# Cross attention and a PReLU layer on one core: small matmul bursts moved to the bank changes, ScalarE's long passes two units apart, batch 1's chain begun in unit 1

## The chip, the cores and the metric

The kernel runs on one core of one Trainium2 chip. The metric is the device time of one execution in microseconds (us), as the median of several runs. All times below are us, unless they are marked ns.

A core has five engines that run side by side and wait for one another by semaphores: TensorE (matmuls, shown as PE, its weight loads as PEld), VectorE (DVE), ScalarE (ACT), GpSimd (POOL) and SyncE (SP, which here only issues DMAs). Each engine works through its own list in order.

## What is computed

Eight batches of cross attention between 512 tokens `x` and 32 states, eight heads of 64, in both directions, and then one layer with a parametric ReLU over all rows:

```python
scores = scale * x @ state.T            # per batch and head: 512 x 32
xread  = softmax(scores) @ state        # the tokens read the states
sread  = softmax(scale * state @ x.T) @ x   # the states read the tokens
rows   = concatenate([xread, sread], axis=2)   # 544 rows of 512 per batch
h      = rows @ w_in                    # d_ff = 2048
g      = maximum(h, 0) + alpha * minimum(h, 0)
out    = g @ w_out
```

Inputs and outputs are float32; the kernel's matmuls take float16.

## The kernel before, in words

**Units.** The main loop (line 546) runs over 128 units, u = 16·b + jc: batch b of 8, block jc of 16 blocks of 128 columns of d_ff. "Relative unit" n of batch b below means u = 16·(b − 1) + n, as in the diff, where the chain of batch b is spread over the units of the batch before. In a unit three things are put into the engines' lists, in this order:

1. `first(b, jc)` (line 363): the first product for the 512 tokens of the batch, two matmuls of 512 columns (L369). `w_in` isn't applied to the token rows: for each batch the product of the states and `w_in`, called m, is made ahead (`state_w_in`, `m_matmuls`, L337, copied by ScalarE, L351), and the softmax weights aT multiply m. Then ScalarE makes `neg`, a relu of −h (L386), and VectorE adds `(1 − alpha)·neg` to h (L391). Its result is gt, the input of the second product. h lies in one of three PSUM buffers (`ps_h`), so a first product waits until the gt of three units before has been made.
2. Some steps of `second` (line 397), the product with `w_out` (L401). Each of a batch's four blocks of 128 tokens, q = 0 to 3, is summed over all 16 jc in a PSUM bank of its own. There are two such banks (`ps_o`), so q = 0 and 1 run together, then 2 and 3. A bank is reused when ScalarE has copied it out (L412, osb); SyncE sends osb to memory. From unit 18 on, a unit holds four matmuls of it, and a pair of banks is finished every eight units, at u = 18, 26, 34 and so on.
3. The side work that `at(u, ...)` has put there (lines 451 to 508): the order is written out by hand.

**The side work of a batch.** `load_x` (GpSimd's DMA, L76); the transpose of x, for batches 0 and 1 by TensorE (`x_transposed_pe`, four transposes and a copy, L167, L170), later by a DMA on SyncE's queue (L158); `scores` (16 small matmuls, L179); for the tokens' softmax `score_blocks` (VectorE transpose, L209), `state_max` (L217), `state_shift` (GpSimd, L223), `state_exp` (ScalarE, L229), `state_sum` (L234, L235), `state_norm` (GpSimd, L238) and `weights_back` (VectorE transpose, L246); for the states' softmax `token_max` (L258, L261), two `token_exp` (ScalarE, L269) and a DMA transpose (L279), `state_reads` (32 small matmuls, L291, and two VectorE operations), `state_reads_transposed` (two transposes, L313, and four VectorE copies into XS, L320); and four `state_w_in`, f = 0 to 3, eight matmuls of 64 rows by 32 columns of weights each. The small matmuls of one such step are called a burst.

**PSUM.** Eight banks: three for h, two for the second product, two as one buffer (`ps_two`) which `scores` and `state_w_in` share, and one (`ps_misc`) for the transposes and state reads. So a `state_w_in` that follows scores waits until both `token_exp` have read them.

**Batch 8.** The states' rows of all batches are the last first product, `first(B, jc)` (L378), four matmuls of 256 columns on XS. In the kernel before, it is done in units 112 to 127, one jc each; after the loop the rest of `second` and `second_reads` (L423) follow.

**Before the loop** (lines 510 to 545) batch 0's chain is done, and GpSimd issues the loads of `w_in` (four parts), `w_out` (four parts) and x(1), x(2) on one queue.

Of the kernel before, what the change touches and what calls it, by code (L numbers as in the profile page):

```python
# [8 lines left out]
F32 = mybir.dt.float32  # L9
# [8 lines left out]
def kernel(  # L18
# [33 lines left out]
    moe = ctx.enter_context(tc.tile_pool(name="moe", bufs=2))  # L52
# [63 lines left out]
    def st_head(b, h):  # L116
        return stT[:, N * (H * b + h) : N * (H * b + h + 1)]
# [72 lines left out]
    def blocks(t):  # L190
        return t.rearrange("p (a n) -> p a n", n=N)

    def over_blocks(t):
        return t.unsqueeze(2).to_broadcast([128, t.shape[1], N])


    def cols(t, j, n):
        return t if j is None else t[:, n * j : n * (j + 1)]
# [22 lines left out]
    def state_shift(b, engine, j=None):  # L221
        ts = blocks(cols(live["ts", b], j, S))
        engine.tensor_tensor(  # L223
            ts, ts, over_blocks(cols(live["mx", b], j, S // N)), ALU.subtract
        )
# [102 lines left out]
    def m_tile(b):  # L328
        if b not in ms:
            ms[b] = moe.tile([128, n_f, 2, 512], F16, name=f"m_{b}", tag="m", bufs=B - 1)  # L330
        return ms[b]

    def m_matmuls(t, b, f, g):
        for k in range(4):
            h = 4 * g + (k ^ g)
            c, r = divmod(h, 2)
            nc.tensor.matmul(  # L337
                t[N * k : N * (k + 1), :],
                st_head(b, h)[64 * r : 64 * r + 64, :],
                w_in_sb[64 * r : 64 * r + 64, c, 512 * f : 512 * (f + 1)],  # L340
                start=True,
                stop=True,
                tile_position=(64 * r, N * k),
                skip_group_check=True,
            )

    def state_w_in(b, f):
# [2 lines left out]
            m_matmuls(t[:, g, :], b, f, g)  # L350
        nc.scalar.copy(m_tile(b)[:, f, :, :], t)  # L351

    def state_w_in_early(b, f):
        ts = [ps_h(f"m_ps{b}_{f}_{g}", [128, 512], F32) for g in range(2)]
        for g in range(2):
            m_matmuls(ts[g], b, f, g)
        for g in range(2):
            nc.scalar.copy(m_tile(b)[:, f, g, :], ts[g])


    gts = {}
# [32 lines left out]

    outs = {}

    def second(b, half, jc):
        for q in (2 * half, 2 * half + 1):
            if jc == 0:
                outs[b, q] = ps_o(f"o_{b}_{q}", [128, d_model], F32)  # L400
            nc.tensor.matmul(  # L401
                outs[b, q],
                gts[b, jc][:, 128 * q : 128 * (q + 1)],
                w_out_sb[:, jc, :],
                start=(jc == 0),
                stop=(jc == n_jc - 1),
            )
        if jc < n_jc - 1:
            return
        for q in (2 * half, 2 * half + 1):  # L410
            osb = moe.tile([128, d_model], F32, name=f"osb_{b}_{q}", tag="osb", bufs=3)
            nc.scalar.copy(osb, outs.pop((b, q)))  # L412
            r, j = divmod(q, 2)
            rows = out[b * S2 : b * S2 + S, :].rearrange("(j p r) d -> r j p d", j=2, r=2)
            nc.sync.dma_start(rows[r, j], osb)


    def second_reads(q):
# [15 lines left out]
            (nc.scalar if i == 0 else nc.sync).dma_start(rows[:, :, w * i : w * (i + 1)], osb)  # L434


    seconds = [(b, half, jc) for b in range(B) for half in range(2) for jc in range(n_jc)]


    def seconds_before(u):  # L440
        if u >= 18:
            return 2 * (u - 10)
        return max(0, u - 3) + (1 if u >= 16 else 0)

    side = {}

    def at(u, fn, *a):
        side.setdefault(u, []).append((fn, a))

    vcopy, acopy = nc.vector.tensor_copy, nc.scalar.copy  # L450
    at(0, states_rest_out, 1)
    at(1, token_exp, 0, 0)
    at(2, token_exp, 0, 1)
    at(3, state_w_in, 0, 2)
    at(5, state_w_in, 1, 0)
    at(4, x_transposed_pe, 1, 0, 0, ps_misc, vcopy)
    at(5, x_transposed_pe, 1, 0, 1, ps_misc, acopy)
    at(6, x_transposed_pe, 1, 1, 0, ps_misc, vcopy)
    at(6, x_transposed_pe, 1, 1, 1, ps_h, acopy)
    at(7, scores, 1)  # L460
    at(8, score_blocks, 1)
    at(9, state_max, 1)
    at(9, state_shift, 1, nc.gpsimd)
    at(9, state_w_in_early, 0, 3)
    at(10, token_max, 1)
    at(11, token_exp, 1, 0)
    at(11, state_exp, 1)
    at(12, token_exp, 1, 1)
    at(12, state_sum, 1)
    at(12, state_norm, 1, nc.gpsimd)  # L470
    at(13, state_w_in, 1, 1)
    at(14, weights_back, 1)
    at(14, token_exp_transposed, 0)
    at(14, x_transposed, 2)
    at(15, state_w_in, 1, 2)
    at(17, token_exp_transposed, 1)
    at(19, state_reads, 0)
    at(21, state_reads_transposed, 0)
    at(22, load_x, 3)
    at(23, state_w_in, 1, 3)  # L480
    for b in range(2, B):
        u = n_jc * (b - 1)
        at(u, scores, b)
        at(u + 1, score_blocks, b)
        at(u + 2, state_max, b)
        at(u + 2, state_shift, b, nc.gpsimd)
        at(u + 3, token_max, b)
        at(u + 4, token_exp, b, 0)
        at(u + 5, state_exp, b)
        at(u + 6, token_exp, b, 1)  # L490
        at(u + 6, state_sum, b)
        at(u + 6, state_norm, b, nc.gpsimd)
        at(u + 7, token_exp_transposed, b)
        if b + 1 < B:
            at(u + 7, x_transposed, b + 1)
        at(u + 9, weights_back, b)
        for f in range(n_f):
            at(u + (9 if b == 2 else 8) + 2 * f, state_w_in, b, f)
        if b == 2:
            at(u + 8, state_reads, 1)  # L500
            at(u + 9, state_reads_transposed, 1)
            at(u + 10, load_x, 4)
        at(u + 11, state_reads, b)
        at(u + 14, state_reads_transposed, b)
        if b + 3 < B:
            at(u + 15, load_x, b + 3)
    for jc in range(n_jc):
        at(n_jc * (B - 1) + jc, first, B, jc)

    states_transposed_first()  # L510
    x_transposed_pe(0, 0, 0, ps_h, vcopy)
# [8 lines left out]
    state_max(0, 1)  # L520
    for f in range(2):
        load_w_in(f)
    load_w_out(0)
    load_w_in(2)
    load_x(1)
    load_w_out(1)
    state_shift(0, nc.gpsimd, 0)
    load_w_in(3)
    load_w_out(2)
    state_shift(0, nc.vector, 1)  # L530
    states_transposed_rest()
    state_exp(0, 0)
    state_exp(0, 1)
    state_w_in_early(0, 0)
    states_rest_out(0)
    state_sum(0, 0)
# [3 lines left out]
    state_sum(0, 1)  # L540
    state_norm(0, nc.vector, 1)
    state_w_in_early(0, 1)
    weights_back(0, 0)
    weights_back(0, 1)
    token_max(0)
    for u in range(n_jc * B):
        first(*divmod(u, n_jc))
        for sec in seconds[seconds_before(u) : seconds_before(u + 1)]:
            second(*sec)
        for fn, args in side.get(u, ()):  # L550
            fn(*args)
    for sec in seconds[seconds_before(n_jc * B) :]:
        second(*sec)
# [32 lines left out]
```

## Time and profile before

| | us |
|---|---|
| median of 3 runs | 245.57 (245.49 to 247.1) |
| the profiled execution | 245.95 |
| its span, first to last instruction | 244.1 |
| TensorE busy | 217.4 (89%) |
| VectorE busy | 170.8 (70%) |
| ScalarE busy | 149.8 (61%) |
| GpSimd busy | 46.1 (19%) |
| second product, L401 | 134.1 in 512 matmuls |
| first product, L369 | 78.6 in 256 matmuls |

A row of a timeline gives start, length, engine, line, operation, result and operands, the shape, and how many instructions are merged in it; in brackets stands how long the engine had been idle and what released it. Matmuls are pipelined: a row's length is longer than the distance from one start to the next, so the distances of starts are what counts. "Clock" is the share of TensorE's full clock that was granted. A table by stage gives, for each stretch of time, the busy time of each engine with the count of its instructions.

### The profile page before, as it was taken

Reading aid. Unit: us, or ns where it says so; the run is one execution under the profiler, and the core shown is the slowest. Engines: PE = TensorE matmul, PEld = TensorE weight load, DVE = VectorE, ACT = ScalarE, POOL = GpSimd, SP = SyncE. Lnnn points to the kernel's source line nnn. Section 1 sums busy time; section 2 is a strip of 40 time slices with the busy share of each in tenths; the row PEclk is TensorE's granted clock in tenths of the full one; section 3 lists DMA queues with packets and bytes.
Section 4 is the critical chain, followed back from the end, with each engine's and each line's share of the span. In section 5 each row is a group of like instructions: output and inputs, shape, how many; then the busy total and the mean of one; then the engine's idle time right before and its main releaser. Section 6 shows DMA issues by size and latency. Waiting matters only on the chain.

```text
span 244.1 us, 4170 instructions
## 1 busy us (share of the span) xinstructions
PE 217.4 (89%) x1632; PEld 97.7 (40%) x1632; DVE 170.8 (70%) x264; ACT 149.8 (61%) x261; POOL 46.1 (19%) x40
## 2 busy tenths in 40 slices
PE   0848867988999999999999999999999999999891
PEld 0513322333344334433444344434443455554381
DVE  0796687779969767977797778787878777673000
ACT  2378766658575965596559665966586675753100
POOL 8850033054203220313031102120212000000000
PEclk9999997999999999999999999999999999999998
DMA  9999997268992358238822602260212020202031
GB/s 79 192 203 195 196 175 89 87 86 119 199 118 86 70 155 78 86 31 192 85 86 45 173 1 86 38 180 0 90 30 99 3 87 0 86 3 83 3 124 51
DMA packets 49363, 23.12 MB, mean 95 GB/s; under 512 B 40512, under 2 KB 45248, under 8 KB 49344
## 3 DMA queue, kind: packets, MB, share of 16 engines
q0 software_dynamic: 20896, 8.62, 28.5%
q1 hardware_dynamic: 26096, 13.96, 21.8%
q10 hardware_dynamic: 2352, 0.27, 0.9%
q8 instruction: 13, 0.21, 0.4%
q14 instruction: 6, 0.05, 0.1%
HBM read 17.31 MB, written 8.91 MB: 107 GB/s over the span
## 4 chain that ended last, share of the span: by engine, by line
PE 65%; DVE 10%; ACT 8%; DMA 6%; issue 5%; POOL 3%; ACTq 0%; DVEq 0%; POOLq 0%
PE o L401 36%; PE h L369 17%; DMA xg<-in_x_dram 6%; ACT osb L412 4%; DVE gt L391 4%; PE m_ps L337 4%; PE o L423 3%; PE h L378 3%; ACT neg L386 2%; PE sc L179 1%; DVE ts L209 1%; DVE nb L258 1%; DVE r L234 1%; DVE mx L217 1%; POOL w_in_sb L98 1%
## 5 line engine op out<-in xcount | busy, mean ns | idle before, releaser
L401 PE MATMUL o<-w_out_sb,gt 128*128 128x512 f16 x512 | 134.1, 381 | 3.5 <-ACT osb L412 2.0
L391 DVE SCALAR_TENSOR_TENSOR gt<-neg,oma_sb,h 128x512 f16<-128x512 f32 x128 | 92.6, 735 | 35.8 <-ACT neg L386 34.8
L386 ACT ACTIVATE neg<-h 128x512 f32<-128x512 f32 (+1 forms) x144 | 82.4, 579 | 40.1 <-PE h L369 29.9
L369 PE MATMUL h<-aT,m 128*128 128x512 f16 x256 | 78.6, 392 | 2.2 <-DVE aT L246 1.7
L401 PEld LDWEIGHTS <-gt 128*128 128x128 f16 x512 | 50.3, 98 | 68.7 <-issue 11.9
L351 ACT CAST m<-m_ps 128x1024 f16<-128x1024 f32 x29 | 29.4, 1013 | 13.8 <-PE m_ps L337 13.3
L369 PEld LDWEIGHTS <-m 128*128 128x128 f16 x256 | 22.0, 99 | 26.7 <-issue 10.1
L223 POOL TENSOR_TENSOR ts<-ts,mx 128x1024 f32<-128x1024 f32 (+1 forms) x8 | 14.4, 1799 | 90.3 <-DVE mx L217 90.3
L412 ACT COPY osb<-o 128x512 f32<-128x512 f32 x32 | 17.2, 595 | 8.3 <-PE o L401 7.8
L238 POOL TENSOR_TENSOR an<-ts,r 128x1024 f16<-128x1024 f32 (+1 forms) x8 | 14.4, 1803 | 37.6 <-DVE r L235 32.9
L337 PE MATMUL m_ps<-w_in_sb,stT 64*32 64x512 f16 x256 | 14.0, 406 | 7.2 <-ACT e L269 5.2
L269 ACT ACTIVATE e<-sc,nb 128x512 f16<-128x512 f32 x16 | 11.1, 692 | 11.2 <-DVE nb L261 11.2
L320 DVE COPY XS<-srT_ps 64x64 f16<-64x64 f16 x32 | 14.1, 439 | 0.6
L337 PEld LDWEIGHTS <-stT 64*32 64x32 f16 x256 | 4.0, 89 | 21.1 <-issue 19.4
L76 POOL DMA_DIRECT2D xg<-in_x_dram x9 | 10.3, 1142 | 10.4 <-PE sr_ps L291 6.3
L433 DVE COPY osr<-o 128x256 f32<-128x256 f32 x2 | 0.8, 424 | 16.2 <-PE o L423 16.2
L391 DVE SCALAR_TENSOR_TENSOR gs<-neg,oma_sb,h 128x256 f16<-128x256 f32 x16 | 7.7, 480 | 5.6 <-ACT neg L386 5.6
L246 DVE STREAM_TRANSPOSE aT<-an 128x1024 f16<-128x1024 f16 (+1 forms) x9 | 10.0, 1119 | 1.7 <-POOL an L238 1.7
L217 DVE TENSOR_REDUCE mx<-ts 128x32 f32<-128x1024 f32 (+1 forms) x9 | 9.8, 1091 | 0.1
L229 ACT ACTIVATE ts<-ts 128x1024 f32<-128x1024 f32 (+1 forms) x9 | 8.6, 959 | 2.0 <-POOL ts L223 1.5
L234 DVE TENSOR_REDUCE r<-ts 128x32 f32<-128x1024 f32 (+1 forms) x9 | 9.8, 1088 | 0.0
L258 DVE TENSOR_REDUCE nb<-sc 128x2 f32<-128x1024 f32 x8 | 9.7, 1210 | 0.0
(41 smaller groups left out, 98.4 us busy)
## 6 DMA issues: line engine op xcount, KB each, us to landing
out_dram<-osb SPq DMA_DIRECT2D x32, 256.0 KB, 2.2
xg<-in_x_dram POOLq DMA_DIRECT2D x7, 512.0 KB, 7.6
w_in_sb<-in_moe_w_in_dram POOLq DMA_DIRECT2D x4, 512.0 KB, 11.1
w_out_sb<-in_moe_w_out_dram POOLq DMA_DIRECT2D x4, 512.0 KB, 18.4
xg<-in_x_dram POOLq DMA_DIRECT2D x2, 256.0 KB, 4.9
out_dram<-osr ACTq DMA_DIRECT2D x2, 128.0 KB, 2.8
out_dram<-osr SPq DMA_DIRECT2D x2, 128.0 KB, 2.8
st<-in_state_dram POOLq DMA_DIRECT2D x1, 224.0 KB, 5.3
```

The lines of the kernel that those rows point to most:

```text
L217: nc.vector.tensor_reduce(cols(live["mx", b], j, S // N), blocks(cols(live["ts", b], j, S)), AX.X, ALU.max)
L223: engine.tensor_tensor(ts, ts, over_blocks(cols(live["mx", b], j, S // N)), ALU.subtract)
L234: nc.vector.tensor_reduce(r1, blocks(cols(live["ts", b], j, S)), AX.X, ALU.add)
L238: engine.tensor_tensor(blocks(cols(live["an", b], j, S)), blocks(cols(live["ts", b], j, S)), over_blocks(cols(live["r1", b], j, S // N)), ...
L320: nc.vector.tensor_copy(XS[64 * r : 64 * r + 64, 2 * g : 2 * g + 2, :, b], t[64 * r : 64 * r + 64, 4 * g + (r ^ g) : 4 * g + 4 : 2, :],)
L337: nc.tensor.matmul(t[N * k : N * (k + 1), :], st_head(b, h)[64 * r : 64 * r + 64, :], w_in_sb[64 * r : 64 * r + 64, c, 512 * f : 512 * (f ...
L351: nc.scalar.copy(m_tile(b)[:, f, :, :], t)
L369: nc.tensor.matmul(h.rearrange("p (r j s) -> p r j s", r=2, j=2), ms[b][:, f, g, 128 * j : 128 * (j + 1)], weights(b, g), start=(g == 0), ...
L386: nc.scalar.activation(neg, h, RELU, bias=0.0, scale=-1.0)
L391: nc.vector.scalar_tensor_tensor(gt, neg, oma_sb[:, jc : jc + 1], h, ALU.mult, ALU.add)
L401: nc.tensor.matmul(outs[b, q], gts[b, jc][:, 128 * q : 128 * (q + 1)], w_out_sb[:, jc, :], start=(jc == 0), stop=(jc == n_jc - 1),)
L412: nc.scalar.copy(osb, outs.pop((b, q)))
```

## The change

- The order of `second`. Before, the two banks of a half took turns by jc. Now `second` does one q and one jc, in the same turns, but for the first and last two jc of a half: there both jc of one q come first, then both of the other. Each q is copied out right after its own last matmul. In the early units the second product starts at unit 7 in place of 3, with two or four matmuls per unit, and has done the same 32 by unit 18.
- The side work of batches 2 to 7 moves within the 16 units: `scores` from relative unit 0 to 1, with `state_reads_transposed` of the batch before right behind it (before: unit 14 of its own 16); `token_max` from 3 to 2; the `token_exp` from 4 and 6 to 3 and 5; `score_blocks` from 1 to 3, `state_max` and `state_shift` from 2 to 4; `state_exp` from 5 to 8; sum and norm from 6 to 10; `weights_back` from 9 to 13; `state_w_in` from 8, 10, 12, 14 to 11, 13, 15 and, for f = 3, to unit 9 of the next 16; `state_reads` from 11 to 13; the DMA transposes from 7 to 6. `load_x` moves by three units.
- Batch 1's chain: its x transposes in units 1 to 3 (before 4 to 6), `scores` in 4 (7), `score_blocks` in 5 (8), and so on; `weights_back` stays in 14. `state_w_in` of batch 0 for f = 2 and 3 is done in halves of four matmuls on `ps_misc`.
- `first(B, jc)` moves two units later, with jc = 13, 14 and 15 all in unit 127.
- On GpSimd's queue x(1) is loaded after the first two parts of `w_in`, ahead of `w_out`, and `w_in`'s last part ahead of batch 0's `state_shift`.

```diff
+    def state_w_in_half(b, f, g, ps_tag):
+        t = ps_tag(f"m_ps{b}_{f}_{g}", [128, 512], F32)
+        m_matmuls(t, b, f, g)
+        nc.scalar.copy(m_tile(b)[:, f, g, :], t)
+
     def state_w_in_early(b, f):
-        ts = [ps_h(f"m_ps{b}_{f}_{g}", [128, 512], F32) for g in range(2)]
         for g in range(2):
-            m_matmuls(ts[g], b, f, g)
-        for g in range(2):
-            nc.scalar.copy(m_tile(b)[:, f, g, :], ts[g])
+            state_w_in_half(b, f, g, ps_h)
...
-    seconds = [(b, half, jc) for b in range(B) for half in range(2) for jc in range(n_jc)]
+    seconds = []
+    for b in range(B):
+        for q in (0, 2):
+            for jc in range(0, n_jc, 2):
+                if jc in (0, n_jc - 2):
+                    seconds += [(b, q, jc), (b, q, jc + 1), (b, q + 1, jc), (b, q + 1, jc + 1)]
+                else:
+                    seconds += [(b, q + i, jc + k) for k in range(2) for i in range(2)]
...
     def seconds_before(u):
         if u >= 18:
-            return 2 * (u - 10)
-        return max(0, u - 3) + (1 if u >= 16 else 0)
+            return 4 * (u - 10)
+        return 32 * max(0, u - 7) // 11 // 2 * 2
...
+    at(1, x_transposed_pe, 1, 0, 0, ps_misc, vcopy)
+    at(2, x_transposed_pe, 1, 0, 1, ps_o, acopy)
     at(2, token_exp, 0, 1)
-    at(3, state_w_in, 0, 2)
-    at(5, state_w_in, 1, 0)
-    at(4, x_transposed_pe, 1, 0, 0, ps_misc, vcopy)
...
-    at(7, scores, 1)
-    at(8, score_blocks, 1)
...
+    at(2, x_transposed_pe, 1, 1, 0, ps_o, vcopy)
+    at(3, x_transposed_pe, 1, 1, 1, ps_misc, acopy)
+    at(4, scores, 1)
+    at(5, state_w_in_half, 0, 2, 0, ps_misc)
+    at(6, state_w_in_half, 0, 2, 1, ps_misc)
+    at(5, score_blocks, 1)
+    at(6, state_max, 1)
+    at(6, state_shift, 1, nc.gpsimd)
+    at(7, token_max, 1)
+    at(8, state_w_in_half, 0, 3, 0, ps_misc)
+    at(9, state_w_in_half, 0, 3, 1, ps_misc)
+    at(9, token_exp, 1, 0)
+    at(10, state_exp, 1)
+    at(11, token_exp, 1, 1)
+    at(11, state_sum, 1)
+    at(11, state_norm, 1, nc.gpsimd)
+    at(13, state_w_in, 1, 0)
     at(14, weights_back, 1)
+    at(15, state_w_in, 1, 1)
...
     for b in range(2, B):
         u = n_jc * (b - 1)
...
+        at(u + 1, scores, b)
+        if b > 2:
+            at(u + 1, state_reads_transposed, b - 1)
+            if b + 2 < B:
+                at(u + 2, load_x, b + 2)
+        at(u + 2, token_max, b)
+        at(u + 3, token_exp, b, 0)
+        at(u + 3, score_blocks, b)
+        at(u + 4, state_max, b)
+        at(u + 4, state_shift, b, nc.gpsimd)
+        at(u + 5, token_exp, b, 1)
+        at(u + 6, token_exp_transposed, b)
         if b + 1 < B:
-            at(u + 7, x_transposed, b + 1)
-        at(u + 9, weights_back, b)
...
+            at(u + 6, x_transposed, b + 1)
+        if b > 2:
+            at(u + 9, state_w_in, b - 1, 3)
+        at(u + 8, state_exp, b)
+        at(u + 10, state_sum, b)
+        at(u + 10, state_norm, b, nc.gpsimd)
         if b == 2:
...
+            at(u + 7, state_w_in, 1, 3)
+            at(u + 9, state_reads, 1)
+            at(u + 10, state_reads_transposed, 1)
+            at(u + 11, load_x, 4)
+        for f in range(3):
+            at(u + 11 + 2 * f, state_w_in, b, f)
+        at(u + 13, state_reads, b)
+        at(u + 13, weights_back, b)
+    u = n_jc * (B - 1)
+    at(u + 1, state_reads_transposed, B - 1)
+    at(u + 9, state_w_in, B - 1, 3)
     for jc in range(n_jc):
-        at(n_jc * (B - 1) + jc, first, B, jc)
+        at(n_jc * (B - 1) + min(jc + 2, n_jc - 1), first, B, jc)
...
     for f in range(2):
         load_w_in(f)
+    load_x(1)
     load_w_out(0)
     load_w_in(2)
-    load_x(1)
+    load_w_in(3)
+    state_shift(0, nc.gpsimd, 0)
     load_w_out(1)
-    state_shift(0, nc.gpsimd, 0)
-    load_w_in(3)
     load_w_out(2)
```

More of the change, by code (lines that the diff above doesn't have):

```diff
@@ L395, with second @@
     outs = {}
[L397 to L407, printed above, removed]
+    def second(b, q, jc):
+        if jc == 0:
+            outs[b, q] = ps_o(f"o_{b}_{q}", [128, d_model], F32)
+        nc.tensor.matmul(
+            outs[b, q],
+            gts[b, jc][:, 128 * q : 128 * (q + 1)],
+            w_out_sb[:, jc, :],
+            start=(jc == 0),
+            stop=(jc == n_jc - 1),
+        )
         if jc < n_jc - 1:
             return
[L410 to L415, printed above, removed]
+        osb = moe.tile([128, d_model], F32, name=f"osb_{b}_{q}", tag="osb", bufs=3)
+        nc.scalar.copy(osb, outs.pop((b, q)))
+        r, j = divmod(q, 2)
+        rows = out[b * S2 : b * S2 + S, :].rearrange("(j p r) d -> r j p d", j=2, r=2)
+        nc.sync.dma_start(rows[r, j], osb)
     def second_reads(q):
@@ L452 @@
     at(1, token_exp, 0, 0)
+    at(1, x_transposed_pe, 1, 0, 0, ps_misc, vcopy)
+    at(2, x_transposed_pe, 1, 0, 1, ps_o, acopy)
     at(2, token_exp, 0, 1)
-    at(3, state_w_in, 0, 2)
-    at(5, state_w_in, 1, 0)
-    at(4, x_transposed_pe, 1, 0, 0, ps_misc, vcopy)
-    at(5, x_transposed_pe, 1, 0, 1, ps_misc, acopy)
-    at(6, x_transposed_pe, 1, 1, 0, ps_misc, vcopy)
-    at(6, x_transposed_pe, 1, 1, 1, ps_h, acopy)
-    at(7, scores, 1)
-    at(8, score_blocks, 1)
[L462 to L471, printed above, removed]
+    at(2, x_transposed_pe, 1, 1, 0, ps_o, vcopy)
[15 more added lines that the diff above has]
+    at(13, state_w_in, 1, 0)
     at(14, weights_back, 1)
+    at(15, state_w_in, 1, 1)
     at(14, token_exp_transposed, 0)
     at(14, x_transposed, 2)
-    at(15, state_w_in, 1, 2)
+    at(16, state_w_in, 1, 2)
     at(17, token_exp_transposed, 1)
@@ L479 @@
     at(22, load_x, 3)
-    at(23, state_w_in, 1, 3)
     for b in range(2, B):
         u = n_jc * (b - 1)
[L483 to L493, printed above, removed]
-        if b + 1 < B:
-            at(u + 7, x_transposed, b + 1)
-        at(u + 9, weights_back, b)
-        for f in range(n_f):
-            at(u + (9 if b == 2 else 8) + 2 * f, state_w_in, b, f)
-        if b == 2:
[L500 to L506, printed above, removed]
+        at(u + 1, scores, b)
[10 more added lines that the diff above has]
+        at(u + 6, token_exp_transposed, b)
+        if b + 1 < B:
+            at(u + 6, x_transposed, b + 1)
[4 more added lines that the diff above has]
+        at(u + 10, state_norm, b, nc.gpsimd)
+        if b == 2:
+            at(u + 7, state_w_in, 1, 3)
[9 more added lines that the diff above has]
+    at(u + 9, state_w_in, B - 1, 3)
     for jc in range(n_jc):
-        at(n_jc * (B - 1) + jc, first, B, jc)
+        at(n_jc * (B - 1) + min(jc + 2, n_jc - 1), first, B, jc)
     states_transposed_first()
```

## The prediction

> **What bounds the kernel now.** I read the table by stage first, cut where the first product of units 0, 18 and 34 starts and then by one batch of 16 units (columns: stretch, length, busy time of TensorE, weight loads, VectorE, ScalarE and GpSimd with counts, granted clock, DMA share, GB/s).
>
> ```profile
> 16.04:44.88 28.84, 23.36 (x156) 9.01 (x157) 20.30 (x28) 20.39 (x36) 3.92 (x3) 0.94 1.13 155
> 44.88:73.14 28.26, 25.51 (x255) 10.76 (x254) 23.76 (x42) 18.52 (x32) 7.28 (x5) 1.00 0.87 131
> ...
> 38.00:40.00 2.00, 2.00 (x13) 0.58 (x6) 1.85 (x3) 1.71 (x3) 0.54 (x1) 0.50 1.58 149
> ...
> 73.14:97.84 24.70, 24.19 (x180) 9.86 (x179) 19.69 (x30) 17.02 (x30) 5.03 (x3) 1.00 0.49 96
> ```
>
> From unit 34 on TensorE is nearly always busy and a batch takes 24.70. Before that, 34 units take 57.1, where the steady pace would need 52.5, although over half of the second product is missing from units 0 to 17. These are two problems, so I read two timelines. First TensorE in the steady part:
>
> ```profile
> 142.43 0.41 PE L337 MATMUL m_ps<-w_in_sb,stT 64*32 64x512 f16 x8
> 142.77 0.28 PE L313 MATMUL srT_ps<-ident,sr 128*128 128x128 f16 x2
> 142.89 0.59 PE L369 MATMUL h<-aT,m 128*128 128x512 f16 x2
> ...
> 144.19 0.59 PE L369 MATMUL h<-aT,m 128*128 128x512 f16 x2
> ...
> 145.57 0.41 PE L179 MATMUL sc<-xT,stT 64*32 64x256 f16 x16
> 145.92 0.60 PE L369 MATMUL h<-aT,m 128*128 128x512 f16 x2
> ...
> 147.22 0.59 PE L369 MATMUL h<-aT,m 128*128 128x512 f16 x2
> ...
> 148.98 0.59 PE L369 MATMUL h<-aT,m 128*128 128x512 f16 x2
> ...
> 158.52 0.59 PE L369 MATMUL h<-aT,m 128*128 128x512 f16 x2
> 159.37 1.30 PE L401 MATMUL o<-w_out_sb,gt 128*128 128x512 f16 x4 [0.26 <-ACT osb L412]
> ...
> 160.94 0.61 PE L369 MATMUL h<-aT,m 128*128 128x512 f16 x2
> ```
>
> A unit with nothing between takes 142.89 to 144.19, 1.30: six matmuls of 0.216. With one burst it takes 1.73 (144.19 to 145.92), so a burst costs 0.44; a second burst right behind another costs 0.12 (142.77 to 142.89). The second product changes its banks in the units at 147.22 and 158.52, relative units 2 and 10 of the next batch's 16: 1.76 without a burst, 2.42 with one, so the two changes cost 0.46 and 0.68. The sum, 16 × 1.2975 + 6 × 0.44 + 0.12 + 1.14 = 24.66, accounts for 24.70. All else is hidden now, but VectorE and ScalarE are not far behind:
>
> ```profile
> 143.09 1.80 DVE L320 COPY XS<-srT_ps 64x64 f16<-64x64 f16 x4
> ...
> 147.86 1.24 DVE L209 STREAM_TRANSPOSE ts<-sc 128x1024 f32<-128x1024 f32 x1
> 149.02 0.70 DVE L391 SCALAR_TENSOR_TENSOR gt<-neg,oma_sb,h 128x512 f16<-128x512 f32 x1
> 149.65 1.21 DVE L217 TENSOR_REDUCE mx<-ts 128x32 f32<-128x1024 f32 x1
> ...
> 151.43 1.22 DVE L258 TENSOR_REDUCE nb<-sc 128x2 f32<-128x1024 f32 x1
> ...
> 152.79 0.73 DVE L391 SCALAR_TENSOR_TENSOR gt<-neg,oma_sb,h 128x512 f16<-128x512 f32 x1
> ```
> ```profile
> 144.82 0.60 ACT L386 ACTIVATE neg<-h 128x512 f32<-128x512 f32 x1 [0.40 <-PE h L369]
> ...
> 147.21 1.07 ACT L412 COPY osb<-o 128x512 f32<-128x512 f32 x2
> ...
> 152.91 0.69 ACT L269 ACTIVATE e<-sc,nb 128x512 f16<-128x512 f32 x1 [1.40 <-DVE nb L261]
> ```
>
> There are three h buffers, so a unit's first product waits for the gt of three units before. Undisturbed, the relu starts 0.63 after the unit's first product (144.19 to 144.82) and gt ends 2.0 after it.
>
> Now the early part, where the chain of waits runs through batch 1's softmax, not through TensorE:
>
> ```profile
> 14.13 0.63 PE L337 MATMUL m_ps<-w_in_sb,stT 64*32 64x512 f16 x8 [1.91 <-DMA w_in_sb<-in_moe_w_in_dram]
> ...
> 16.04 3.59 PE L369 MATMUL h<-aT,m 128*128 128x512 f16 x8 [1.27 <-DVE aT L246]
> ...
> 22.64 0.40 PE L167 MATMUL xT_ps<-ident,xg 128*128 128x128 f16 x4 [0.20 <-DMA xg<-in_x_dram]
> ...
> 28.70 0.59 PE L369 MATMUL h<-aT,m 128*128 128x512 f16 x2
> ...
> 37.74 0.63 PE L337 MATMUL m_ps<-w_in_sb,stT 64*32 64x512 f16 x8 [3.25 <-ACT e L269]
> ...
> 42.71 0.59 PE L369 MATMUL h<-aT,m 128*128 128x512 f16 x2 [0.47 <-DVE aT L246]
> ```
> ```profile
> 37.72 1.21 DVE L234 TENSOR_REDUCE r<-ts 128x32 f32<-128x1024 f32 x1
> ...
> 41.41 1.25 DVE L246 STREAM_TRANSPOSE aT<-an 128x1024 f16<-128x1024 f16 x1 [0.66 <-POOL an L238]
> ```
> ```profile
> 39.47 1.91 POOL L238 TENSOR_TENSOR an<-ts,r 128x1024 f16<-128x1024 f32 x1 [4.71 <-ACT m L351]
> ```
>
> TensorE stands still for 3.25 in unit 13, because m_ps shares its banks with the scores that token_exp still reads; after it the clock is 0.50, and matmuls take twice as long until about 41. Unit 16, the first of batch 1, starts at 42.71 when the weights come back.
>
> **The change, part by part.** *Steady bank changes.* After it, the last two matmuls of a bank come before the last two of the other bank, and a burst (relative units 1 and 9) and a first product follow before the banks are needed: 0.43 + 0.44 + 0.43 = 1.30. The bank needs 0.17 for the last matmul to end, 0.60 for the copy (147.21, half of x2 plus overlap) and 0.1 of signals: 0.87. The second copy ends 0.48 later and its bank is needed 0.43 later. In unit 9 the copies queue behind state_exp of unit 8; placing the ScalarE rows one after another leaves 0.15 of cover. So I take 0 for both: 1.14 saved per batch. Without cover, 0.5 per batch comes back.
>
> *Bursts.* The state_reads burst now stands right behind an m_ps burst (unit 13). By the row at 142.77 a follower is cheaper; it is 32 matmuls here and not two, so I take 0.35 in place of 0.44 (bounds 0.12 and 0.44): 0.09 saved. Scores followed by the transposes cost 0.55, as their parts now.
>
> The Trainium skill, TensorEngine Tiling (Array Packing), Key Properties, speaks against moving bursts around: a change of the tiling mode, not merely of the tile, drains TensorE. By it state_reads (128×32) behind m_ps (64×32) would pay in full, 0.44, and the gain below would be 0.5 smaller over six batches; this case's 142.77 row, where the follower goes into the very mode that is needed next, cannot tell.
>
> *VectorE in the steady part.* XS copies (unit 1), token_max (2), score transpose (3) and state_max (4) now follow each other, four units in a row, where the XS copies stood two units ahead of the rest before. Time from unit 1's start, first products at 0, 1.85, 3.15, 4.45, 5.74, 7.04, 8.34, 9.64 (units 1 to 8). VectorE: gt1 to 2.0, XS 2.05 to 3.9, gt2 to 4.5, token_max to 5.9 (151.43 to 152.79 is 1.36), gt3 to 6.5, transpose to 7.7 (1.16), gt4 to 8.4, state_max to 9.45, gt5 to 10.2. Unit 7 waits 0.1 for gt4, unit 8 another 0.5 for gt5: 0.6 lost per batch (bounds 0 and 1.3, if each of the seven steps were 0.1 longer). The relus of units 4 to 6 wait on ScalarE behind token_exp, which waits for token_max; they are done before VectorE gets to them, so this costs nothing more. The new period is 20.76 + 3 × 0.44 + 0.79 + 0.55 + 0.6 = 24.02, 0.68 less; five batches (units 34 to 114): **−3.4**, between 0 and −6.4.
>
> *Units 0 to 18.* Eight loads land between 14.13 (w_in's second) and x(2):
>
> ```profile
> 37.34 1.62 SPq L158 DMA_TRANSPOSE xT<-xg  x1
> ...
> SPq L158 <- DMA xg<-in_x_dram: 14.9, 1, 14.9
> ...
> DMA to landing us min/median/max: 3.9/3.9/5.0
> ```
> ```profile
> 18.60 0.61 ACT L386 ACTIVATE neg<-h 128x512 f32<-128x512 f32 x1
> ```
>
> So 2.9 each, as the three up to 22.64 confirm. x(1), third now, lands near 17.0; w_in's third at 22.8 and fourth at 25.7; w_out's four at 19.9 to 34.4, before their units; x(2) stays at 37.3. Units 0 and 1 run to 17.75 at 0.43 a matmul (3.59 for eight). ScalarE goes from the relu at 18.60 through two token_exp, two relus and two copies of x(1), about 0.5 to 0.9 each, to 22.5; scores(1) end at 22.9. Units 5 to 10 start at 22.9, 23.8, 25.05, 25.95, 27.2 and 28.95; the half bursts on one shared bank cost two waits of 0.4 for its copy. VectorE: score transpose 24.8 to 26.0, state_max to 27.75, token_max to 29.75, gt8 at 30.45, each with a gt between; unit 11 waits 0.7 for gt8. ScalarE: token_exp from 29.8, relu, state_exp to 32.05, relu to 32.6. VectorE: gt11 to 33.35, sum and reciprocal (37.72 to GpSimd's start at 39.47 less a gt: 1.4) to 34.75; GpSimd 1.91, to 36.7; weights back 38.0. Unit 16 starts at 38.05 in place of 42.71, units 16 and 17 end at 40.65, and scores(2) now wait for x(2)'s transpose: 37.34 + 3.9 = 41.2. Unit 18 starts at 41.65 in place of 44.88: **−3.2**, between −1.2 (landing 5.0, another 0.9 on VectorE) and −3.8 (no DMA wait).
>
> *Units 18 to 34.* Units 16 × 1.2975, bursts: five alone 0.44 and 0.11 twice, the pair 0.79, the pair 0.55: 24.54; VectorE is late again, by the same rows, at unit 25 (0.62): 25.16 in place of 28.26: **−3.1**, between −2.2 and −3.7.
>
> *The last batch.* XS of batch 7 is written from unit 114's start + 0.55 (behind gt113) for 1.8; the first state product, now in unit 114, wants it at + 1.30 and waits about 1.0. One m_ps burst (f = 3) moved in: 0.44. **+1.4**, between +0.4 and +1.6. The three state products at the end of unit 127 are the same work, later.
>
> ```profile
> 221.32 1.89 PE L401 MATMUL o<-w_out_sb,gt 128*128 128x512 f16 x8
> 223.67 7.34 PE L401 MATMUL o<-w_out_sb,gt 128*128 128x512 f16 x32 [0.46 <-ACT osb L412]
> ...
> 231.96 7.04 PE L423 MATMUL o<-w_out_sb,gs 128*128 128x256 f16 x63 [0.22 <-ACT osb L412]
> ```
>
> At the end, with no burst between, the first bank's copy starts two matmuls (0.43) earlier, at both changes: **−0.8**, between −0.3 and −1.0.
>
> Sum: −3.2 − 3.1 − 3.4 + 1.4 − 0.8 = −9.1. The profiled execution took 245.95 (span 244.1 and 1.85 around it), 0.38 above the median; 236.85 on its scale is 236.5 on the median's.
>
> **The rivals.**
> *VectorE keeps up* (for it: the 0.6 is a difference of two long sums; against: all durations are rows): the waits for gt in six batches and half of that for XS go, 4.1: 232.4.
> *The early chain gains half* (for it: units 5 to 16 hang on three engines in turn, and each new wait shifts the rest; against: scores(1) surely come earlier, as their load does): +3.2: 239.7.
> *The bursts don't cover the change* (for it: only 0.15 of cover in unit 9, and copies behind any late ScalarE pass arrive late; against: units 1 and 9 hold no pass of 1 us): 0.5 over six batches, 239.5.
> *VectorE falls further behind*: each later gt delays the next products, so 1.8 per batch in place of 0.6: +7.2, 243.7, no change.
> *Slower: half clock early.* Units 3 to 17 hold 15 × 0.43 + 32 × 0.216 and 3.6 of bursts, 17.0 of TensorE's work, in 21.5. If the lighter units 3 to 9, without the second product, kept the clock at 0.50 as after the 3.25 wait, a share s of this work costs 17 s − 4.5; from s = 0.8 the whole gain is gone, at s = 1 the time is 249.0. Against: before, units 4 to 12 had two of second's matmuls each, hardly more, and at 28.70 a unit's first product takes 0.59 for two, full pace.
> The Trainium skill, TensorE: Matmul & The Clock Gate, Part 1, puts the drop to half rate after about 3.4 us of idleness and the return after as long a busy stretch; the 3.25 wait and the 0.50 agree roughly, and by this rule no wait forecast here, all under 1, brings the drop.
>
> **How the numbers follow.** Forecast 0.60 (own range 234 to 239), VectorE keeps up 0.13, early half 0.11, no cover 0.05, VectorE further behind 0.07, half clock 0.04. The range 231.8 to 241.2 leaves out the last two. A change of 1% is about what a measurement can tell: faster 0.89, same 0.07, slower 0.04.
>
> **What would show it.** Right: no wait of o for osb from unit 18 to 113, units 2 and 10 at 1.30 and batch period near 24.0; TensorE waiting for gt about 0.5 in relative unit 8; unit 16 near 38, unit 18 near 41.7 behind a DMA; clock 1.00 from 21 on; a wait of 1 for XS near unit 114. Wrong: a period still at 24.7, unit 18 after 43.5, or matmuls 0.43 apart after unit 4.

## The result, and the profile after

| | before | after |
|---|---|---|
| median (lowest to highest) | 245.91 (245.49 to 247.1) | 239.54 (238.97 to 240.42) |
| profiled execution | 245.95 | 238.97 |
| its span | 244.1 | 237.0 |

The ratio is 0.9736, with a 95% interval of 0.9689 to 0.9783: 6.4 less in the median, 7.0 in the profiled executions. The forecast was 9.1 less. (The median of before is over four runs here, one more than in the table ahead of the prediction.)

The table by stage of the changed kernel, cut at the same units (the first product of units 0, 18 and 34, and one batch from unit 34; columns as before), and the two microseconds in which the clock had been at 0.50:

```profile
15.99:41.54 25.55, 22.24 (x157) 8.90 (x157) 20.62 (x29) 20.94 (x39) 3.92 (x3) 1.00 1.16 175
41.54:67.68 26.14, 24.91 (x254) 10.67 (x247) 22.33 (x38) 17.46 (x30) 7.28 (x5) 1.00 0.75 119
38.00:40.00 2.00, 1.90 (x15) 0.71 (x15) 1.31 (x3) 1.27 (x3) 0.00 (x0) 1.00 1.23 176
67.68:92.01 24.33, 23.74 (x181) 9.97 (x180) 19.57 (x30) 17.13 (x30) 5.03 (x3) 1.00 0.74 122
```

Units 0 to 18 take 25.55 in place of 28.84, units 18 to 34 26.14 in place of 28.26, a batch 24.33 in place of 24.70. The clock no longer falls, and the pace of the matmuls agrees: the two of unit 16 take 0.43 together (38.10 to 38.53). TensorE's timeline of a steady batch (relative unit 2 starts at 140.66, unit 7 at 147.56, unit 10 at 152.37):

```profile
140.66 0.59 PE L371 MATMUL h<-aT,m 128*128 128x512 f16 x2
...
141.95 0.59 PE L371 MATMUL h<-aT,m 128*128 128x512 f16 x2
...
145.84 0.59 PE L371 MATMUL h<-aT,m 128*128 128x512 f16 x2
...
147.56 0.59 PE L371 MATMUL h<-aT,m 128*128 128x512 f16 x2 [0.27 <-DVE gt L393]
...
149.34 0.59 PE L371 MATMUL h<-aT,m 128*128 128x512 f16 x2 [0.33 <-DVE gt L393]
...
152.37 0.60 PE L371 MATMUL h<-aT,m 128*128 128x512 f16 x2
...
153.67 0.59 PE L371 MATMUL h<-aT,m 128*128 128x512 f16 x2
...
158.10 0.41 PE L337 MATMUL m_ps<-w_in_sb,stT 64*32 64x512 f16 x8
158.44 0.42 PE L291 MATMUL sr_ps<-xg,e2T 128*32 128x64 f16 x32
158.79 0.61 PE L371 MATMUL h<-aT,m 128*128 128x512 f16 x2
```

The units of the bank changes, 2 and 10, take 1.29 and 1.30: both waits are gone. In their place TensorE waits for gt in units 7 and 8: 145.84 to 147.56 is 1.72, 147.56 to 149.34 is 1.78, so 0.42 and 0.48 above a plain unit. (The bracket gives only the part in which no earlier matmul was still draining.) That is 0.9 per batch. Why gt is late is seen on VectorE and then on ScalarE, in the same batch:

```profile
140.86 1.81 DVE L320 COPY XS<-srT_ps 64x64 f16<-64x64 f16 x4
...
143.36 1.22 DVE L258 TENSOR_REDUCE nb<-sc 128x2 f32<-128x1024 f32 x1
...
145.63 1.25 DVE L209 STREAM_TRANSPOSE ts<-sc 128x1024 f32<-128x1024 f32 x1 [0.20 <-ACT e L269]
...
147.43 1.21 DVE L217 TENSOR_REDUCE mx<-ts 128x32 f32<-128x1024 f32 x1
```
```profile
144.82 0.69 ACT L269 ACTIVATE e<-sc,nb 128x512 f16<-128x512 f32 x1 [1.64 <-DVE nb L261]
...
146.91 0.69 ACT L269 ACTIVATE e<-sc,nb 128x512 f16<-128x512 f32 x1 [0.34 <-DVE ts L209]
```

The four long steps stand in a row as forecast. But the score transpose also waits for the first token_exp, and the second token_exp for the transpose: the two engines read the scores in turns.

From the rest of the span, in order: unit 16, scores of batch 2, unit 25, the first state product, and the last bank change.

```profile
38.10 0.59 PE L371 MATMUL h<-aT,m 128*128 128x512 f16 x2 [0.98 <-DVE aT L246]
...
41.20 0.41 PE L179 MATMUL sc<-xT,stT 64*32 64x256 f16 x16 [0.33 <-DMA xT<-xg]
...
50.72 0.59 PE L371 MATMUL h<-aT,m 128*128 128x512 f16 x2
...
53.22 0.59 PE L371 MATMUL h<-aT,m 128*128 128x512 f16 x2 [1.04 <-DVE gt L393]
...
191.24 0.38 PE L380 MATMUL h<-XS,w_in_sb 128*128 128x256 f16 x2 [0.53 <-DVE XS L320]
...
217.47 7.12 PE L402 MATMUL o<-w_out_sb,gt 128*128 128x512 f16 x32 [0.24 <-ACT osb L412]
```

Unit 25 starts 2.50 after unit 24, 1.20 late. Its cause stands in unit 19, on ScalarE and on VectorE:

```profile
46.20 0.69 ACT L269 ACTIVATE e<-sc,nb 128x512 f16<-128x512 f32 x1 [2.12 <-DVE sr L302]
```
```profile
47.01 1.25 DVE L209 STREAM_TRANSPOSE ts<-sc 128x1024 f32<-128x1024 f32 x1 [0.85 <-ACT e L269]
```

Here token_exp of batch 2 does not wait for token_max, done by 44.9, but for the VectorE part of state_reads of batch 0 (L302).

### The profile page after: what moved, and what is told of

The parts are those of the page before. It is cut to its first block, busy times and chain, and to the rows that moved or that the text cites. A ratio compares the mean times of both kernels' runs of the same rounds, so it can differ in the third digit from the quotient of the medians.

```text
span 237.0 us, 4171 instructions
## 1 busy us (share of the span) xinstructions
PE 214.0 (90%) x1632; PEld 97.8 (41%) x1632; DVE 170.2 (72%) x264; ACT 150.0 (63%) x262; POOL 46.2 (20%) x40
## 4 chain that ended last, share of the span: by engine, by line
PE 71%; DVE 17%; ACT 4%; DMA 4%; issue 2%; POOL 0%; ACTq 0%; POOLq 0%
PE o L402 37%; PE h L371 21%; DVE gt L393 5%; DVE ts L209 4%; PE m_ps L337 4%; DVE mx L217 4%; PE o L423 3%; PE h L380 3%; DMA xg<-in_x_dram 2%; DMA xT<-xg 2%; ACT neg L388 1%; DVE XS L320 1%; PE sc L179 1%; PE sr_ps L291 1%; ACT e L269 1%
## 5 line engine op out<-in xcount | busy, mean ns | idle before, releaser
L402 PE MATMUL o<-w_out_sb,gt 128*128 128x512 f16 x512 | 130.6, 379 | 0.2 <-ACT osb L412 0.2
L371 PE MATMUL h<-aT,m 128*128 128x512 f16 x256 | 77.6, 386 | 7.4 <-DVE gt L393 4.8
L351 ACT CAST m<-m_ps 128x1024 f16<-128x1024 f32 x28 | 28.5, 1018 | 12.5 <-PE m_ps L337 12.5
L209 DVE STREAM_TRANSPOSE ts<-sc 128x1024 f32<-128x1024 f32 x7 | 8.7, 1249 | 1.8 <-ACT e L269 1.8
L380 PE MATMUL h<-XS,w_in_sb 128*128 128x256 f16 x64 | 9.5, 273 | 0.5 <-DVE XS L320 0.5
```

Source lines behind the costliest of these rows:

```text
L209: nc.vector.transpose(live["ts", b], sc.rearrange("p r j g s -> p (r j g s)"))
L371: nc.tensor.matmul(h.rearrange("p (r j s) -> p r j s", r=2, j=2), ms[b][:, f, g, 128 * j : 128 * (j + 1)], weights(b, g), start=(g == 0), ...
L380: nc.tensor.matmul(h, w_in_sb[:, c, 128 * jc : 128 * (jc + 1)], XS[:, c, :, :].rearrange("p n b -> p (n b)"), start=(c == 0), stop=(c == n ...
L402: nc.tensor.matmul(outs[b, q], gts[b, jc][:, 128 * q : 128 * (q + 1)], w_out_sb[:, jc, :], start=(jc == 0), stop=(jc == n_jc - 1),)
```

## The experiments

Each was timed beside the kernel before on the same chip; its own median of before is given where it matters.

**1. XS copies back to relative unit 15** (`e1_xs_at_15`).

```diff
-            at(u + 1, state_reads_transposed, b - 1)
...
         at(u + 13, weights_back, b)
+        at(u + 15, state_reads_transposed, b)
...
-    at(u + 1, state_reads_transposed, B - 1)
```

> The changed kernel with state_reads_transposed of batches 2 to 7 moved from relative unit 17 (one into the next 16) back to 15, behind the state_w_in burst there, so that its four XS copies no longer stand ahead of token_max, score transpose and state_max. Theory (VectorE's row of four long steps holds back gt): the waits of 0.42 and 0.48 in relative units 7 and 8 fall to about 0.1 together, the period from 24.33 to about 23.5, and the wait for XS near unit 114 (0.87) goes; 5 x 0.8 + 0.9 = 4.9 less, about 234.6. Rival (the waits come from score transpose and token_exp taking turns on the scores alone, the XS copies are covered): the period stays near 24.3 and only the 0.87 goes, about 238.6.

Measured: 234.64, ratio 0.9551 (0.9526 to 0.9575). The table by stage gives one batch, and the timeline its units 7 and 8:

```profile
135.53:159.08 23.55, 23.55 (x180) 9.97 (x179) 19.48 (x30) 17.15 (x29) 3.83 (x2) 1.00 0.28 79
```
```profile
145.04 0.59 PE L371 MATMUL h<-aT,m 128*128 128x512 f16 x2
...
146.48 0.59 PE L371 MATMUL h<-aT,m 128*128 128x512 f16 x2
```

Unit 7 takes 1.44, so 0.14 of the 0.9 is left; the period is 23.55 and TensorE has no idle time in it. The wait for XS near unit 114 is gone too. The theory held. The score transpose still waits for token_exp here, so the turns alone do not hold gt back: the length of VectorE's row does. This version is faster than both kernels.

**2. Score transpose ahead of the first token_exp** (`e2_blocks_first`).

```diff
-        at(u + 3, token_exp, b, 0)
         at(u + 3, score_blocks, b)
+        at(u + 3, token_exp, b, 0)
```

> The changed kernel with score_blocks put ahead of the first token_exp in relative unit 3, nothing else. Theory (ScalarE and VectorE read the same PSUM tile of scores one after the other, in the order in which they were put into the lists): VectorE's transpose no longer waits for token_exp, but token_exp now waits for the transpose, the relu of relative unit 4 stands behind it on ScalarE, and gt4 and gt5 come 1.1 later than now; waits in units 7 and 8 together 2.0 in place of 0.9, period about 25.4, about 245. Rival (the two can overlap, and the wait seen is only the order of the lists): the transpose starts 0.3 earlier, token_exp as early as now, the waits fall to 0.6, about 238.

Measured: 245.76, ratio 1.0000 (0.9977 to 1.0023): one exchanged pair of lines loses the whole gain of the change. From the table of waits and from TensorE's timeline (unit 7):

```profile
ACT e L269 <- DVE ts L209: 20.5, 6, 3.4
PE h L371 <- DVE gt L393: 11.2, 13, 1.4
```
```profile
149.70 0.59 PE L371 MATMUL h<-aT,m 128*128 128x512 f16 x2
...
152.59 0.59 PE L371 MATMUL h<-aT,m 128*128 128x512 f16 x2 [1.43 <-DVE gt L393]
```

ScalarE now stands idle for up to 3.4 ahead of token_exp, until the transpose is done (in the change it was 1.64, until token_max was done); the relus stand behind token_exp, and unit 7 starts 1.59 late. The two readers do take turns, in the order of the lists; the rival fell.

**3. The new order of the second product alone, on the kernel before** (`e3_order_alone`).

```diff
-                if jc in (0, n_jc - 2):
+                if jc == n_jc - 2 or (jc == 0 and (b, q) != (0, 0)):
...
-        return 32 * max(0, u - 7) // 11 // 2 * 2
+        return 2 * (max(0, u - 3) + (1 if u >= 16 else 0))
```

(The lines that are taken out are those of the change; all the rest is the kernel before.)

> The kernel before with the new order of the last two and first two jc at each bank change alone (not in batch 0's first half); no burst is moved. Theory (it is the burst and the first product between that cover the copy; the order gives only one matmul, 0.22): the two changes per batch cost about 0.25 and 0.46 in place of 0.46 and 0.68, at the end 0.5 is saved: 3.1 less than before in all, about 242.8. Rival (the order does most of it): the changes cost under 0.1 each, 7 less, about 239.

Measured: 243.97, ratio 0.9921 (0.9894 to 0.9949). TensorE's timeline, relative units 2, 9 and 10 starting at 147.32, 156.91 and 158.62:

```profile
147.32 0.59 PE L369 MATMUL h<-aT,m 128*128 128x512 f16 x2
...
148.71 0.59 PE L369 MATMUL h<-aT,m 128*128 128x512 f16 x2
...
156.91 0.60 PE L369 MATMUL h<-aT,m 128*128 128x512 f16 x2
...
158.62 0.59 PE L369 MATMUL h<-aT,m 128*128 128x512 f16 x2 [0.24 <-DVE gt L391]
...
160.62 0.60 PE L369 MATMUL h<-aT,m 128*128 128x512 f16 x2
```

Neither theory had it right. The bank changes cost 0.09 (147.32 to 148.71) and 0.26 (158.62 to 160.62, less 1.30 and a burst), down from 0.46 and 0.68, so the order does more than one matmul of cover: a likely reason is that it gives one before the change and one after, where the second bank is needed a matmul later. But 0.41 comes back in unit 9 as a wait for gt. The waits for the bank had covered VectorE's lag.

**4. The bursts at the bank changes, the banks taking turns as before** (`e4_turns`).

```diff
-                if jc in (0, n_jc - 2):
-                    seconds += [(b, q, jc), (b, q, jc + 1), (b, q + 1, jc), (b, q + 1, jc + 1)]
-                else:
-                    seconds += [(b, q + i, jc + k) for k in range(2) for i in range(2)]
+                seconds += [(b, q + i, jc + k) for k in range(2) for i in range(2)]
```

> The changed kernel with the two banks taking turns throughout, as before, and all else as changed: the bursts alone at the bank changes. Theory (the bursts cover the copies): waits for osb from unit 18 to 113 stay under 0.1 per change, at the end of the kernel 0.6 is lost; about 240.3. Rival (the order does most of it): about 0.3 to 0.5 per change come back, 243 to 245.

Measured: 241.1, ratio 0.9815 (0.9788 to 0.9841). Unit 10 in TensorE's timeline:

```profile
152.91 0.60 PE L371 MATMUL h<-aT,m 128*128 128x512 f16 x2
...
154.40 0.59 PE L371 MATMUL h<-aT,m 128*128 128x512 f16 x2
```

It takes 1.49, so 0.19 of the change is uncovered, twice what was expected; unit 2 has no wait. The bursts alone take away 0.95 of 1.14 per batch, the order alone 0.79. Each nearly suffices, and together they leave nothing.

**5. state_reads of batch 0 in unit 16** (`e5_reads_16`, on top of experiment 1).

```diff
-    at(19, state_reads, 0)
+    at(16, state_reads, 0)
```

> The first experiment's kernel (XS copies at relative unit 15) with state_reads of batch 0 moved from unit 19 to 16, nothing else. Theory (in unit 19 token_exp of batch 2 writes its sums into the buffer that state_reads of batch 0 still has to read, so ScalarE waits 2.1 for VectorE, and the score transpose and gt22 behind it hold up unit 25 by 1.2): token_exp starts about 1.2 earlier, unit 25 waits 0.2 or less; 1.2 less than the first experiment, about 233.4. Rival (unit 25 waits because batch 0's XS copies stand in the same row): the wait stays over 0.8, about 234.4.

Measured: 233.51, ratio 0.9473 (0.9427 to 0.9518). On the chip of experiment 1 it takes 233.55 (run 10), 1.1 less than experiment 1. token_exp of batch 2 starts right behind token_max, at 45.05 in place of 46.20. Units 24 and 25:

```profile
49.98 0.61 PE L371 MATMUL h<-aT,m 128*128 128x512 f16 x2
...
52.09 0.59 PE L371 MATMUL h<-aT,m 128*128 128x512 f16 x2 [0.64 <-DVE gt L393]
```

The wait for state_reads was there, but 0.8 of unit 25's wait stayed, where 0.2 was forecast. So the rival is right in part. That the time came out near the expected 1.2 is in part luck: units 18 to 34 take 24.88 in place of 26.13, and only 0.8 of this 1.25 are waits that went. The rest is the burst of state_reads itself: unit 19 takes 1.29 in place of 1.74, as the burst now runs in unit 16, ahead of scores(2), which cannot start before x(2)'s transpose lands anyway (unit 18 starts no later, 41.65 for 41.79).

**6. Batch 0's XS copies in unit 18 too** (`e6_reads_16_back_18`).

```diff
-    at(21, state_reads_transposed, 0)
+    at(18, state_reads_transposed, 0)
```

> As the run before, with state_reads_transposed of batch 0 moved from unit 21 to 18 too. Theory: the row of steps is short already, 0 to 0.2 less than the run before, about 233.3. Rival (the XS copies are what holds up unit 25): 1.2 less than the first experiment only here, and not in the run before.

Measured: 234.59, ratio 0.9518 (0.9468 to 0.9568), 1.1 more than experiment 5. Both theories fell. In unit 18 the copies stand ahead of token_max, as they do in the changed kernel's steady part, and ScalarE waits for it, then TensorE for gt, in units 22 and 23:

```profile
46.99 0.69 ACT L269 ACTIVATE e<-sc,nb 128x512 f16<-128x512 f32 x1 [2.57 <-DVE nb L261]
```
```profile
47.66 0.59 PE L371 MATMUL h<-aT,m 128*128 128x512 f16 x2 [0.42 <-DVE gt L393]
...
49.73 0.59 PE L371 MATMUL h<-aT,m 128*128 128x512 f16 x2 [0.62 <-DVE gt L393]
```

Unit 25 waits for nothing there; units 22 and 23 start 0.58 and 0.77 later than a plain unit would. So 1.8 of VectorE's work costs most when it stands directly ahead of the row. That asked for a place behind it (run 9).

**7. The early part alone, on the kernel before** (`e7_early_alone`): the lines of the change for units 0 to 17 and for the loads; the side work from batch 2's chain on and the order of the second product stay.

```diff
-        return max(0, u - 3) + (1 if u >= 16 else 0)
+        return 16 * max(0, u - 7) // 11
...
+    load_x(1)
     load_w_out(0)
```

> The kernel before with the change's units 0 to 17 and its order of loads alone: batch 1's chain begun in unit 1, second from unit 7 on with the banks taking turns, everything from batch 2's chain on as before (so scores of batch 2 in unit 16). Theory (the early chain is worth what unit 18 comes earlier, and x(2)'s transpose, there at 41.2, is the floor): unit 16 starts near 38.1, scores(2) wait in it until 41.2, unit 18 starts near 42.9 in place of 44.88, and no more is won behind it: 2.0 less than before, about 243.7. Rival (what is won early is lost again behind unit 18 on VectorE): 245 to 246.

Measured: 243.7, ratio 0.9882 (0.9841 to 0.9922). Scores of batch 2 and unit 18 in TensorE's timeline:

```profile
41.41 0.41 PE L179 MATMUL sc<-xT,stT 64*32 64x256 f16 x16 [1.71 <-DMA xT<-xg]
...
43.05 0.59 PE L371 MATMUL h<-aT,m 128*128 128x512 f16 x2
```

As expected, x(2)'s transpose is the floor: unit 18 starts at 43.05 in place of 44.88, 1.8 earlier. The medians give 2.9 less than before on this chip (246.57), with an interval of 1.9 to 3.9. The changed kernel reaches unit 18 another 1.5 earlier (41.54): there scores(2) stand in unit 17, and TensorE does the products of unit 17 while the transpose runs.

**8. The loads in the order of before** (`e8_load_order`).

```diff
     for f in range(2):
         load_w_in(f)
-    load_x(1)
     load_w_out(0)
     load_w_in(2)
-    load_w_in(3)
-    state_shift(0, nc.gpsimd, 0)
+    load_x(1)
     load_w_out(1)
+    state_shift(0, nc.gpsimd, 0)
+    load_w_in(3)
```

> The changed kernel with the loads on GpSimd's queue in the order of before, x(1) fifth and not third. Theory (the early chain begins with x(1)): the transposes of unit 1 wait until x(1) lands near 22.6, TensorE's list behind them stands still for 5, unit 16 starts near 42.5, unit 18 near 45; 3.5 more than the changed kernel, about 243. Rival (the chain is set by ScalarE and VectorE anyway, and x(1) need not be early): under 1 more, 240.5 at most.

Measured: 244.06, ratio 0.9889 (0.9847 to 0.9931). The transposes of unit 1, two matmuls behind them, and unit 16:

```profile
23.16 0.61 PE L167 MATMUL xT_ps<-ident,xg 128*128 128x128 f16 x4 [5.33 <-DMA xg<-in_x_dram]
...
25.27 1.06 PE L371 MATMUL h<-aT,m 128*128 128x512 f16 x2
26.13 0.63 PE L167 MATMUL xT_ps<-ident,xg 128*128 128x128 f16 x4
...
43.57 0.59 PE L371 MATMUL h<-aT,m 128*128 128x512 f16 x2 [0.98 <-DVE aT L246]
```

TensorE stands still for 5.33, and its matmuls behind the wait stand about 0.43 apart until about 28 (two take 25.27 to 26.13), twice the later distance. Unit 16 starts 5.5 later than in the changed kernel, and unit 18 at 46.61, later than before (44.88). Without the early load, batch 1's chain begun in unit 1 is worth nothing.

**9. Batch 0's XS copies in unit 23, behind batch 2's row** (`e9_back_23`), and **10. experiment 5 timed again beside it** (`e10_e5_again`).

```diff
-    at(21, state_reads_transposed, 0)
+    at(23, state_reads_transposed, 0)
```

> XS copies of batches 2 to 7 at relative unit 15, state_reads of batch 0 in unit 16, and state_reads_transposed of batch 0 in unit 23, behind state_max of batch 2 (unit 20) and not ahead of token_max as in unit 18 or between as in unit 21. Theory (what counts is where the 1.8 of XS copies stand in VectorE's list against batch 2's row of token_max, transpose and state_max): behind the row they delay only gt24, which nothing waits for soon, so the wait of 0.8 left in unit 25 with state_reads in unit 16 goes, and nothing comes in its place: 0.8 less than that run, about 232.7. Rival (the row alone makes unit 25 wait, wherever the copies stand): 233.5, no change.

> The kernel with state_reads of batch 0 in unit 16 and its XS copies still in unit 21, timed again beside the run before on the same chip: 233.5 by both theories, 0.8 above the run before by the theory and level with it by the rival.

Measured: 234.11, ratio 0.9505 (0.9482 to 0.9528), and 233.55, ratio 0.9492 (0.9469 to 0.9514). Units 24 and 25 of the first, and scores of batch 3:

```profile
50.96 0.60 PE L371 MATMUL h<-aT,m 128*128 128x512 f16 x2
...
52.26 0.59 PE L371 MATMUL h<-aT,m 128*128 128x512 f16 x2
...
68.72 0.41 PE L179 MATMUL sc<-xT,stT 64*32 64x256 f16 x16 [1.83 <-DMA xT<-xg]
```

Unit 25's wait is gone (1.30), so the place of the copies was its cause, but the time did not fall: scores(3) wait 1.83 for the transpose of x(3). The profiled execution, at 235.99, was the longest of the six; how much of the wait the others have is not known.

**11 and 12. x(3) loaded in unit 17**, with the copies in unit 23 (`e11_back_23_load_17`) and in 21 (`e12_back_21_load_17`).

```diff
+    at(17, load_x, 3)
     at(17, token_exp_transposed, 1)
...
-    at(22, load_x, 3)
```

> The kernel with XS copies of batch 0 in unit 23, and load_x of batch 3 moved from unit 22 to 17, which state_reads in unit 16 allows. Theory (the copies behind the row did free unit 25, and what took its place was x(3): loaded from 51.8, landed 59.9, its transpose then shared the DMA engines with the load of x(4) and took 8.8, so scores of batch 3 waited 1.8): x(3) is there before its transpose is asked for, scores(3) wait for nothing, unit 25 waits for nothing: 0.8 less than the run with batch 0's copies in unit 21, about 232.7. Rival (unit 25's gain is lost elsewhere than in the DMA): 233.5 to 234.

> The same early load of x(3) with batch 0's XS copies left in unit 21. Both theories: unit 25 still waits 0.8, nothing waits for x(3): 233.5, as without the early load; the difference to the run before is what the place of the copies is worth, 0.8 by the theory, nothing by the rival.

Measured: 233.29, ratio 0.947 (0.9434 to 0.9505), and 233.56, ratio 0.9484 (0.9451 to 0.9517). Nothing waits for x(3) in either. Units 24 and 25 in the first and in the second:

```profile
50.30 0.61 PE L371 MATMUL h<-aT,m 128*128 128x512 f16 x2
...
51.61 0.59 PE L371 MATMUL h<-aT,m 128*128 128x512 f16 x2
```
```profile
50.41 0.60 PE L371 MATMUL h<-aT,m 128*128 128x512 f16 x2
...
52.51 0.59 PE L371 MATMUL h<-aT,m 128*128 128x512 f16 x2 [0.64 <-DVE gt L393]
```

By the rows the place is worth its 0.8 in unit 25, but 0.3 of it comes back in unit 26 (1.72 in place of 1.42), where the transposes of batch 1's state reads wait for VectorE, which is still behind; units 18 to 34 take 24.42 in place of 24.88. The medians differ by 0.3, in the same direction, and the intervals overlap, so the times alone do not settle it. The first has the lowest median here: 13 less than the kernel before on its chip (246.35).

## Why the prediction was right or wrong

The direction, the place of each gain and the stalls that would replace them came out; the total was 2 to 3 too large, and 239.54 lies above the forecast's own range of 234 to 239. Term by term, in spans:

| term | forecast | measured |
|---|---|---|
| units 0 to 18 | −3.2 | 25.55 − 28.84 = −3.3 |
| units 18 to 34 | −3.1 | 26.14 − 28.26 = −2.1 |
| five steady batches | −3.4 | 5 × (24.33 − 24.70) = −1.9 |
| the last batch | +1.4 | +1.3 |
| the end | −0.8 | −1.1 |

The last two are cut at the matmuls that were before at 221.32 and are now at 215.34: from unit 34 to there 148.18 became 147.66, −0.5, of which the batches are −1.9, and from there to the end 22.78 became 21.66. Units 18 to 34 and the end lie just outside their bounds, the one for the worse and the other for the better. (The terms of units 18 to 34 add up to 24.52 and not 24.54, which changes nothing.)

**Right: units 0 to 18.** Unit 16 was forecast at 38.05 and starts at 38.10; scores(2) were to wait for x(2)'s transpose until 41.2 and start at 41.20. Run 8 confirms one end of this chain, x(1)'s load, and run 7 the other, x(2)'s transpose.

**Right: the bank changes and the bursts.** The waits went to zero, and the cover of only 0.15 in unit 9 held. That the bursts are what covers is half the truth: by run 3 the order alone does more than half. The follower burst, taken as 0.35, takes 0.35 (158.44 to 158.79) and not the full 0.44.

**Wrong in size: VectorE's lag.** The step that failed is the sentence that token_exp's wait on ScalarE "costs nothing more". It was worked out for the relus behind token_exp; the score transpose stands behind it as well, because ScalarE and VectorE read the scores in turns (run 2). It starts 6.8 after unit 1 (138.80 to 145.63) and not 6.5. With that, gt4 and gt5 come 0.3 later: unit 8 waits 0.48 as forecast (0.5), but unit 7 waits 0.42 in place of 0.1, and the period is 24.33 in place of 24.02. This 0.3 is read from the rows; no run takes away this one wait alone. At unit 25 the same row costs 1.2, and 0.3 in unit 23, in place of 0.62: there token_exp waited in addition for state_reads of batch 0, which the prediction did not look for. Run 5 takes that part away, 0.7 of the 1.5 in units 23 to 25; the remaining 0.8 goes with the place of batch 0's XS copies (run 11). The two misses make 2.5 (1.5 in the steady batches, 1.0 in units 18 to 34); the end, the early units and the last batch gave 0.5 back, so the spans fell by 7.1 in place of 9.1.

The Trainium skill, PSUM — Partial Sum Buffer, Terms, states that two engines on one bank and quadrant at the same time are a collision, reads against reads included. The waits here fit a program that is built to keep them apart: VectorE waits 1.8 for token_exp ahead of six of the changed kernel's score transposes, and in run 2 six waits of ScalarE, 20.5 in all, end with the transpose. No run here lets the two overlap, so what the chip would do is not shown.

**The rivals.** By the number alone "the early chain gains half" (239.7) and "no cover" (239.5) would be right, but neither happened, and the match is luck: units 0 to 34 gained 5.4 of the 6.3 forecast, and both waits at the bank changes went to zero. By the mechanism "VectorE further behind" was the near one: 0.9 per batch, between the forecast's 0.6 and its 1.8. The half clock did not happen either: from unit 3 on (19.76) a pair of first-product matmuls lasts 0.59, as at full pace.

The Trainium skill, TensorE: Matmul & The Clock Gate, Part 1, lets the rate fall after about 3.4 us of idleness: here the longest wait after unit 1 is near 1, and no row shows the clock fall. In run 8 TensorE waited 5.33, and its matmuls were slow behind it, but they had been as slow ahead of it, so that run shows no fall either.

## What to carry to other kernels

When a wait of the busiest engine is taken away, look at once for the engine that was late behind it: here the waits for the bank had covered VectorE's lag, and 0.9 of the 1.14 us per batch went into it until 1.8 us of copies were no longer put directly ahead of the row of long steps (run 1). Write such a row down with every wait of its steps, those on the other engine that reads the same PSUM tile and on buffers that turn over included; a pair of lines exchanged there was worth 6 us. Here the chain begun earlier was worth nothing until its load was moved too (run 8). A burst of the busiest engine costs least where that engine would wait for a DMA anyway (run 5).

## What the runs showed of the hardware

- A DMA transpose of one batch of x lands 3.9 after its issue in the median of the changed kernel, and 5.3 at most; in run 9, where the next load of x was issued 0.06 before it (59.82 and 59.88), it took 8.8. The two stand on different queues (SyncE's and GpSimd's). That the load caused this fits the order of the issues, but no run changed this alone.
- A burst of state_reads right behind one of state_w_in costs 0.35 and not 0.44, although the two differ in tiling (128×32 behind 64×32).
- The clock column can read 1.00 while matmuls run at half pace: in the changed kernel from 16 to 18, where the four from 15.99 to 17.67 stand 0.42 apart, and in run 8 from 24 to 28, where a pair takes about 0.86 (25.27 to 26.13), against 0.43 later. The distance of the starts is the surer sign.
